# The PSUM tiles of a woven attention and Fourier stage in other banks

## The chip, the cores and the metric

The kernel runs on one core of a Trainium2 chip. The metric is the device time of one execution in microseconds (us); smaller is better. "Before" is the kernel as it stands, "after" the same kernel with the change described below.

## The reference, cut to what matters

Two results are put side by side in the output. Part A is a segmented attention with a memory (32 heads of width 18, four segments of 512 positions); part B takes the real part of a two-dimensional Fourier transform, written as products with cosine and sine matrices.

```
q, k, v = x @ wq, x @ wk, x @ wv           # [2048, 576], 32 heads x 18, 4 segments x 512
for each segment s:
    a_dot = softmax(causal(q_s k_s^T * 18**-0.5)) @ v_s
    a_mem = (phi(q_s) @ M) / (phi(q_s) @ z + 1e-6)
    out_s = sigmoid(beta) * a_mem + (1 - sigmoid(beta)) * a_dot
    M += phi(k_s)^T v_s ;  z += sum phi(k_s)
A = out @ wo
B = Cr @ (xB @ Hr^T) - Ci @ (xB @ Hi^T)    # [2048, 576]
result = concat(A, B)
```

## The kernel before, in words

The kernel has three stages, and the order of the instructions on each engine is the order in which the program records them (no scheduler moves them). Float32 operands are split into a high and a low half, so that a product takes three matmuls for each block of 128.

**Stage 1** (the loop over `s`, four segments) makes q, k and v of each segment, looks up the memory and adds to it. Its PSUM pool takes all eight banks. Banks 0 to 2 hold the sums of the memory (`m_ps`); they are read for the last time by `memory()` at the start of the last segment (L372, L374) and stand empty from there on. The five other banks, 3 to 7, are five buffers of one tag, `acc`, taken in turn by the products of q, k (L250, L84), v (L84) and by the lookups.

A lookup (`lookup(s, j)`, one for each of the four position tiles `j` of a segment) uses two of these banks. The first one, `o`, takes nine small matmuls (L396), goes to SBUF by ACT (L397) and is read a last time by DVE (L407). The second one, `u`, takes three matmuls (L402 to L404), is read by ACT (L405, L406) and by DVE (L408 to L410), and then serves as scratch for the denominators: DVE adds 1e-6 (L413), takes the reciprocal (L414) and multiplies by the gate (L415). Only when L415 has run is the bank free. GpSimd then forms the result (L417).

**Stage 2**, the woven stage, opens a second PSUM pool when the first one is closed. Its tiles wait for what used their bank before, tile by tile (`reuse_waits="tile"`), and not for the whole pool. It weaves two streams into one: `dense()`, the Fourier products, and `attention()`, which is cut into eight slots per pair of heads with a planned length each (`SLOTS`). After every slot of the attention the loop draws so many Fourier products that both streams get through at the same rate.

- Fourier: `hidden(ri, tt)` (L622 to L627) makes one product of 14 matmuls for each half of the columns, into a tile `d` of 128 x 288. Three banks take turns for `d`. ACT takes the high half out (L628), and one tick later DVE the low half (recorded at L94, since it is put off with `later`). `product()` and `sequence()` (matmuls at L577) come after the 16 tiles of `hidden`. The operands are cut from a loaded chunk: ACT makes `chi` (L451) and `xtail` (L453); one tick later `clo` (L456) and the low part of `xtail` (L458) are made, by GpSimd, except for the first two chunks, which DVE does.
- Attention: `scores` (L738) fills a tile `s` for a pair of rows of the score matrix, and `smallest` masks it and finds the largest score (L744: a custom DVE instruction, followed by a small one that reads its accumulator). `s` has two banks in turn (`s0`, `s1`), `t` two (`t0`, `t1`) and `pv` one.

The program thus takes its first steps in stage 2 in this order on PE: the first score of head 0 (512 columns), the first `d` product of 14 matmuls, six matmuls of the second `d` product, the second score of head 0 (two matmuls of 128 and 384 columns), the eight matmuls left of the second product, the third score (256 columns), the third and fourth `d` products (14 matmuls each, chunk 1), and then the fifth (chunk 2, whose `clo` is GpSimd's).

Which bank a tag gets is settled when a tile of it is first made: the pool gives the lowest free ones. Before the change the two lines ahead of `EDGE` make two `s` tiles that nobody uses, so that `s` comes first. The built program has them so; the right column tells the last user of the bank in stage 1 and its last reader:

| bank | before | last user in stage 1, last reader |
|---|---|---|
| 0, 1, 2 | `s`, `s`, `d` (1st product) | sums of the memory, read at the start of segment 3 |
| 3 | `d` (3rd product) | v of tile 3, second half; DVE L327 |
| 4 | `d` (2nd product) | `u` of the lookup of tile 3, the last of the stage; DVE L415 |
| 5 | `t`, also `trm` | v of tile 3, first half; DVE L327 |
| 6 | `t` | `u` of the lookup of tile 2; DVE L415 |
| 7 | `pv` | `o` of the lookup of tile 3; DVE L407 |

## Time and profile before

| what | value |
|---|---|
| median of 3 runs | 1001.27 us (1000.71 to 1001.88) |
| the profiled execution's own time | 1002.62 us |
| DMA | 209 GB/s on average, 208.92 MB |
| share of the chain that ended last, by engine | PE 85%, DVE 5%, ACT 4% |

The profile is of one execution. Its span runs from the first to the last instruction and is 1.7 us shorter than the execution's own time (1002.62 - 1000.9). PE is the matmul engine, PEld its weight loads, DVE VectorE, ACT ScalarE, POOL GpSimd, SP the queue that issues nearly all DMAs. A row of the timeline gives the start in us from the start of the span, the duration, the engine, the line of the code and the tiles (written <- read); in brackets stands how long the engine was idle before, and what the profile takes for the end of that idle time.

### The profile page before, as it was taken

The numbers are of one execution on the slowest core, as the hardware profiler recorded it, in microseconds if no ns is written. First come the engines' busy times: TensorE is split into PE (matmuls) and PEld (weight loads), VectorE is DVE, ScalarE is ACT, GpSimd is POOL, SyncE is SP. The second block draws the span as 40 slices with busy tenths as digits, with TensorE's granted clock in tenths as the row PEclk, the third lists the DMA queues.
The fourth block names the chain that finished last, engine by engine and source line by source line (L and its number), as shares of the span: only waits on it lengthen the run. The fifth ranks groups of instructions, "written<-read, shape, count | busy, mean of one in ns | idle before, by whom it ended". The sixth has DMA issues, their size and how long they took to land.

```text
span 1000.9 us, 25591 instructions
## 1 busy us (share of the span) xinstructions
PE 990.0 (99%) x9294; PEld 925.6 (92%) x9294; DVE 752.7 (75%) x2052; ACT 712.3 (71%) x1680; POOL 635.9 (64%) x700
## 2 busy tenths in 40 slices
PE   9999999989999999999999999999999999999998
PEld 8989989889999999999999999999999999999998
DVE  6557667594678777878898888898888899998321
ACT  7757575653887787878778788877767777777243
POOL 2657576675767667666766776776767767767000
PEclk9999999999999999999999999999999999999999
DMA  7537456767588999899999987889999999989455
GB/s 248 185 117 252 178 176 244 233 231 217 143 186 211 219 240 227 203 236 220 249 220 238 218 218 191 180 203 233 226 227 213 233 237 247 248 188 200 127 150 139
DMA packets 305614, 208.92 MB, mean 209 GB/s; under 512 B 206288, under 2 KB 260432, under 8 KB 305488
## 3 DMA queue, kind: packets, MB, share of 16 engines
q1 hardware_dynamic: 305248, 207.15, 81.0%
q8 instruction: 73, 1.20, 0.5%
q14 instruction: 53, 0.43, 0.2%
q10 hardware_dynamic: 240, 0.14, 0.0%
HBM read 121.32 MB, written 57.93 MB: 179 GB/s over the span
## 4 chain that ended last, share of the span: by engine, by line
PE 85%; DVE 5%; ACT 4%; issue 2%; POOL 1%; DMA 1%; SPq 0%; POOLq 0%; DVEq 0%; ACTq 0%
PE d L577 38%; PE s L738 7%; PE d L84 6%; PE v L84 4%; PE pv L856 4%; PE qk L250 4%; PE d L622 3%; PE d L623 3%; PE d L624 3%; PE pv L857 2%; PE m L363 1%; PE t L812 1%; PE qk L84 1%; DMA craw<-cT 1%; DVE r L276 1%
## 5 line engine op out<-in xcount | busy, mean ns | idle before, releaser
L744 DVE CUSTOM_DVE_ANT_0 s<-s,causal 128x128 f32<-128x128 f32 (+3 forms) x512 | 249.7, 498 | 103.2 <-PE s L738 94.1
L456 POOL TENSOR_TENSOR clo<-craw,chi 128x512 fp32r<-128x512 f32 x158 | 216.8, 1372 | 100.0 <-ACT chi L451 73.1
L577 PE MATMUL d<-wide,chi 128*128 128x288 f32 x1408 | 266.2, 306 | 0.4 <-DVE y L647 0.4
L577 PEld LDWEIGHTS d<-wide,chi 128*128 128x128 f32 x1408 | 211.8, 189 | 3.2 <-issue 0.9
L577 PE MATMUL d<-wide,clo 128*128 128x288 f32 x704 | 177.5, 319 | 0.0
L778 POOL TENSOR_TENSOR hl<-pf,hl 128x768 f16<-128x768 f32 x64 | 112.9, 1764 | 68.6 <-ACT hl L774 55.3
L824 ACT ACTIVATE phi<-t 128x384 f16<-128x384 f32 x128 | 61.7, 482 | 103.4 <-PE t L821 103.3
L738 PE MATMUL s<-ks,qs 108*128 108x128 bf16 (+3 forms) x512 | 133.9, 304 | 1.3 <-ACT pf L767 0.8
L767 ACT ACTIVATE pf<-s,nb 128x128 f32<-128x128 f32 (+3 forms) x256 | 128.3, 527 | 6.2
L839 DVE TENSOR_TENSOR plo<-pf,phi 128x384 f16<-128x384 f32 (+1 forms) x128 | 126.4, 987 | 0.0
L577 PE MATMUL d<-ab,chi 128*128 128x288 f32 x640 | 126.0, 306 | 0.0
L577 PEld LDWEIGHTS d<-wide,clo 128*128 128x128 f32 x704 | 118.6, 189 | 1.6
L825 ACT ACTIVATE pf<-t 128x384 f32<-128x384 f32 (+1 forms) x192 | 99.5, 518 | 6.1 <-PE t L812 5.9
L451 ACT ACTIVATE chi<-craw 128x512 fp32r<-128x512 f32 x160 | 100.1, 626 | 4.1 <-DMA craw<-cT 2.2
L577 PEld LDWEIGHTS d<-ab,chi 128*128 128x128 f32 x640 | 98.5, 189 | 0.6
L774 ACT ACTIVATE hl<-pf 128x768 f16<-128x768 f32 (+1 forms) x128 | 87.4, 729 | 2.0
L622 PE MATMUL d<-wide,chi 128*128 128x288 f32 x256 | 84.8, 331 | 2.8 <-ACT xtail L453 2.8
L577 PE MATMUL d<-ab,clo 128*128 128x288 f32 x320 | 84.8, 314 | 0.0
L623 PE MATMUL d<-wide,chi 128*128 128x288 f32 x256 | 76.1, 297 | 0.0
L624 PE MATMUL d<-wide,clo 128*128 128x288 f32 x256 | 76.0, 297 | 0.0
L778 DVE TENSOR_TENSOR hl<-pf,hl 128x512 f16<-128x512 f32 x64 | 67.7, 1058 | 0.1
L839 POOL TENSOR_TENSOR plo<-pf,phi 128x384 f16<-128x384 f32 x64 | 59.4, 928 | 12.9 <-ACT pf L825 10.3
(214 smaller groups left out, 2500.0 us busy)
## 6 DMA issues: line engine op xcount, KB each, us to landing
craw<-cT SPq DMA_DIRECT2D x128, 256.0 KB
ks<-kd SPq DMA_DIRECT2D x32, 432.0 KB
qs<-qd SPq DMA_DIRECT2D x32, 432.0 KB
craw<-xtT SPq DMA_DIRECT2D x32, 320.0 KB
vd<-vs SPq DMA_DIRECT2D x16, 440.0 KB
vst<-vd SPq DMA_DIRECT2D x32, 220.0 KB
qd<-p SPq DMA_DIRECT2D x16, 384.0 KB
kd<-p SPq DMA_DIRECT2D x16, 384.0 KB
```

The costliest lines, as they stand in the source:

```text
L84: pe.matmul(o, a, b, start=n == 0, stop=n == len(terms) - 1)
L451: act.activation(hi, raw[:, :4], AF.Copy)
L456: engine.tensor_tensor(lo, raw[:, :4], hi.bitcast(F32), OP.subtract)
L577: pe.matmul(o[h], a, b[:, h * 288:h * 288 + 288], start=start, stop=stop)
L622: pe.matmul(o, xh[:, k], wl[k][:, cs], start=k == 0, stop=False)
L623: pe.matmul(o, xh[:, k], wh[k][:, cs], start=False, stop=False)
L624: pe.matmul(o, xl[:, k], wh[k][:, cs], start=False, stop=False)
L738: pe.matmul(o[:, c:c + w], q[:, i * P:w], k[:, :w], start=True, stop=True)
L744: dve.tensor_tensor_reduce(o[:, c:c + w], o[:, c:c + w], CAUSAL[0][:, L - w:], scale=scale, scalar=-LOWEST, op0=OP.add, op1=OP.min, accum_ ...
L767: act.activation(f[:, FIRST_COL[i]:FIRST_COL[i] + w], o[:, c:c + w], AF.Exp, bias=nb[:, i:i + 1], scale=-1.0)
L778: engine.tensor_tensor(hl[:, 1, a:b], f[:, a:b], hl[:, 0, a:b], OP.subtract)
L839: (pool if kind == 2 else dve).tensor_tensor(lo[:, a:b], f[:, a:b], hi[:, a:b], OP.subtract)
```

## The change

Unused tiles of the other tags are made ahead of the two unused `s` tiles, so that the pool hands out its banks in another order. Nothing else changes: the built program has the same instructions in the same order on every engine and in every queue.

```
+    ps.tile([P, 288], F32, name="d", bufs=3)
+    for tag in "tt":
+        bank("t", [P, L], F32, tag)
+    ps.tile([P, 448], F32, name="pv", bufs=1)
     for _ in range(2):
         bank("s", [P, L], F32, "s")
```

`bank` gives the two buffers of a tag in turn; since it is called twice for each tag, the turn afterwards is as it was. In the built program the banks then stand so: `d` in 0 (first product), 2 (second) and 1 (third), `t` in 3 (also `trm`) and 4, `pv` in 5, `s` in 6 (first score) and 7 (second score). The waits of five PE instructions differ:

| PE instruction | waited before for | waits after for |
|---|---|---|
| first score, its weight load | its operands' loads | those, and the last readers of bank 6 (ACT L406, DVE L415 of the lookup of tile 2) |
| second `d` product, first matmul | the last readers of bank 4 (ACT L406, DVE L415 of the lookup of tile 3) | nothing |
| second score, first matmul | nothing | the last reader of bank 7 (DVE L407 of the lookup of tile 3) |
| `trm`, at 243.7 us of the span | its operands | those, and a product of stage 1 on PE itself |
| a score after `trm` | nothing | a lookup of stage 1 on PE itself |

## The prediction

> **What bounds the kernel now.** The page first: the busy shares, and the granted clock in 40 slices.

> ```profile
> span 1000.9 us, 25591 instructions
> PE 990.0 (99%) x9294; PEld 925.6 (92%) x9294; DVE 752.7 (75%) x2052; ACT 712.3 (71%) x1680; POOL 635.9 (64%) x700
> PEclk9999999999999999999999999999999999999999
> ```

> PE is busy all the time and the next engine at 75%. So a change that gives PE the same instructions in the same order can move the end in two ways alone: by PE's waits, and by the speed at which its matmuls run. The waits of PE are few; the second view lists all of them.

> ```profile
> engine line waited for: us in total, times, longest us
> PE d L622 <- ACT xtail L453: 2.8, 1, 2.8
> PE warm L239 <- DVE ones L68: 1.1, 1, 1.1
> PE s L738 <- ACT pf L767: 0.8, 1, 0.8
> PE d L577 <- DVE y L647: 0.4, 1, 0.4
> PE s L738 <- DVE negm L744: 0.4, 2, 0.2
> PE kt L305 <- ACT kf L271: 0.4, 2, 0.2
> ```

> Half of what PE waits for is one wait, 2.8 us, before a Fourier product, and none is for a DMA. The timeline shows it at the seam of the two stages:

> ```profile
> 219.00 0.28 PE L404 MATMUL look<-md,pq_hi 128*128 128x152 f32 x1
> 219.11 0.39 PE L738 MATMUL s<-ks,qs 108*128 108x512 bf16 x1
> ...
> 220.94 0.30 PE L626 MATMUL d<-wide,xtail 128*128 128x288 f32 x1
> ...
> 221.07 0.29 PE L627 MATMUL d<-wide,xtail 128*128 128x288 f32 x1
> ...
> 222.25 0.20 DVE L407 TENSOR_TENSOR nd<-nd,look 128x57 f32<-128x57 f32 x1
> ...
> 223.78 0.30 ACT L453 ACTIVATE xtail<-craw 128x128 fp32r<-128x128 f32 x1
> ```

> ```profile
> 223.84 0.19 DVE L415 TENSOR_TENSOR w<-look,g 128x32 f32<-128x32 f32 x1
> ...
> 224.18 0.37 PE L622 MATMUL d<-wide,chi 128*128 128x288 f32 x1 [2.81 <-ACT xtail L453]
> ...
> 224.58 0.14 DVE L744 DVE_READ_ACCUMULATOR2_ANT negm<- 128x1 f32 x1
> ...
> 225.05 0.49 PE L738 MATMUL s<-ks,qs 108*128 108x128 bf16 x2
> ```

> The first product ends at 221.36 (221.07 + 0.29), the second one starts at 224.18. The profile names ACT's `xtail`, because that instruction ends last (224.08). But it is of the next chunk, which this product does not read. What the product waits for by the program is bank 4, and that is free when DVE's L415 ends, at 224.03. From there to PE's start are 0.15 us; I use that as the handoff to PE throughout.

> The second cost is in the table by stretches (last columns: granted clock, DMA share, GB/s):

> ```profile
> 224.00:225.00 1.00, 0.82 (x6) 0.83 (x6) 0.72 (x3) 0.08 (x1) 0.83 (x1) 1.00 0.00 0
> 225.00:226.00 1.00, 1.00 (x7) 0.95 (x6) 0.39 (x3) 0.00 (x0) 1.00 (x2) 0.61 0.07 16
> 226.00:227.00 1.00, 1.00 (x6) 1.00 (x5) 0.91 (x3) 0.00 (x0) 0.94 (x2) 0.50 0.78 288
> 227.00:228.00 1.00, 1.00 (x6) 0.85 (x6) 0.26 (x1) 0.41 (x1) 0.92 (x2) 0.50 0.65 253
> 228.00:229.00 1.00, 1.00 (x7) 1.00 (x7) 0.54 (x3) 0.00 (x0) 0.92 (x1) 0.68 1.04 225
> 229.00:232.00 3.00, 3.00 (x25) 3.00 (x23) 0.46 (x1) 1.20 (x4) 1.34 (x2) 1.00 0.94 293
> ```

> A microsecond after the gap the clock is at half speed, for 0.39 + 0.50 + 0.50 + 0.32 = **1.71 us** of lost full-speed time (the shares missing to 1.00). So the gap costs 2.81 + 1.71, about 4.5 us, 0.45% of the span. That is all that is at stake.

> **The change part by part.** Nothing is added, removed or moved on any engine or queue. Only waits change.

> *Removed: the wait of the second product.* Its new bank, 2, has been empty for the whole segment. PE would go on at 221.20 (221.07 plus the spacing of 0.13 that the rows at 220.94 and 221.07 show). For more matmuls I take the spacing from these two starts, 14 products apart:

> ```profile
> 229.86 0.29 PE L622 MATMUL d<-wide,chi 128*128 128x288 f32 x1
> ...
> 231.73 0.29 PE L622 MATMUL d<-wide,chi 128*128 128x288 f32 x1
> ```

> (231.73 - 229.86) / 14 = 0.1336 us, or 0.46 ns a column. 231.73 is also the start of the fifth product, the mark at which I compare.

> *Added: the first score waits for bank 6.* All of PE is queued behind it.

> ```profile
> 215.40 0.25 ACT L406 ACTIVATE nd<-look 128x76 f32<-128x76 f32 x1
> ...
> 217.41 0.19 DVE L415 TENSOR_TENSOR w<-look,g 128x32 f32<-128x32 f32 x1
> ```

> The bank's last readers end at 215.65 and 217.60, and the score starts at 219.11: met 1.5 us earlier. Cost 0; it would take a DVE late by more than 1.5 us to cost anything.

> *Added: the second score waits for bank 7.* Six matmuls of the second product run from 221.20 to 222.00. Then the score needs DVE's L407, which ends at 222.45; with the handoff PE starts at 222.60. **A wait of 0.60.** Behind it stand eight Fourier matmuls and everything else on PE. It can't be longer by much, since DVE's row does not depend on anything that moves, nor much shorter: 0.50 with a handoff of 0.05.

> *What is late next: the third score.* It waited for the reading of the first score already, and never had to. Now: 222.60 + 0.24 (512 columns) + 8 x 0.1336 = 223.91. But the first score's maximum is read by DVE at 224.58 to 224.72, behind the whole of the last lookup; plus 0.15 is 224.87. **A wait of 0.96.** So the two new waits together bring PE back to what held it before, DVE's queue; but by then PE is through with 14 products and two scores, where before it had done six products.

> *Then.* 224.87 + 0.12 (256 columns) + 28 x 0.1336 = 228.73 for the start of the fifth product. Its third matmul, at 229.00, needs `clo` of chunk 2 from GpSimd:

> ```profile
> 227.64 1.28 POOL L456 TENSOR_TENSOR clo<-craw,chi 128x512 fp32r<-128x512 f32 x1
> ```

> That ends at 228.92, and GpSimd's chain up to there hangs on L415, not on PE, so that it does not move: 229.07, **a wait of 0.07**. The fifth product in effect starts at 228.80, where before it was 231.73: **2.93 us earlier**. In terms of its causes: 2.81 less 1.63 of new waits is 1.2, and 1.7 is the clock, if it stays whole.

> The GpSimd term can be worse, as DVE now runs its masks and the first low half about 0.8 us sooner beside it. The nearest rows for such a meeting:

> ```profile
> 217.52 0.68 DVE L456 TENSOR_TENSOR clo<-craw,chi 128x512 fp32r<-128x512 f32 x1
> ...
> 219.41 1.64 DVE L456 TENSOR_TENSOR clo<-craw,chi 128x512 fp32r<-128x512 f32 x1
> ```

> The same instruction took 0.96 more where GpSimd's L336 ran beside it. What DVE moves here reads PSUM and ran beside GpSimd before as well, so I take 0 and keep 0.96 for the range; below nothing there is no reason. With handoffs of 0.05 in place of 0.15 at the three waits the gain is 0.3 more.

> *`trm` and the score behind it* wait for PE's own count, for products 20 us old. A count that PE has to look at by itself took this:

> ```profile
> L622 PEldq EVENT_SEMAPHORE  x1: 51/51/51, 224.1 to 224.1; - x1
> ```

> Here it rides on the matmul; 0 to 0.05 us each, and I take 0. Two such separate counts stand at the seam before and after.

> **Does it stay to the end?** No later wait of PE in the list is for a DMA, and where ACT cuts the chunks that feed PE it waited for the load only twice:

> ```profile
> ACT chi L451 <- DMA craw<-cT: 2.2, 2, 1.8
> ```

> All engines get their work about 3 us sooner, in the same order, so the other waits move along. Sum for the profiled execution: 1002.62 - 2.93 = 999.69 (span 1000.9 to about 998.0). The runs shown have a median 1.35 below it, so **1001.27 - 2.93 = 998.3 us**.

> **The rivals.**

> *The clock is cut all the same (B).* After the change PE rests 0.60 and 0.96 us within 2.9 us. For: the 2.81 us in one piece did it, with products running for the last microsecond before the cut. Against: the next longest wait within the run, 0.8 us, did not, and the mean granted clock says that no other did:

> ```profile
> core 0: 1000.9 us, clock 0.998
> ```

> (1 - 0.998) x 1000.9 is 2.0 us lost, and 1.71 of it are accounted for. 1.56 in two pieces lies nearer to 0.8 than to 2.81. If it is cut, 1.71 is lost among the 28 matmuls and the wait of 0.07 goes: gain 2.93 + 0.07 - 1.71 = 1.29, **1000.0 us**.

> *The timed runs before had no cut (C).* The cut began at 225.2, where nothing in the kernel happens. If its place is fixed by something outside, the gap may fall elsewhere in other executions. Then before itself reaches the fifth product at 224.18 + 0.07 (the slower first matmul) + 42 x 0.1336 + 0.36 = 230.22, and the gain is 230.22 - 228.80 = 1.42: **999.9 us**. The three runs before are 1.2 us apart, which neither shows nor excludes it.

> [...]

> *The gain is handed back (E).* PE is ahead of its loads for a while; if the DMA queue, at shares of 0.94 to 1.04 at 228 to 232 us, can't bring later chunks sooner, PE waits for them instead. Then up to 2.93 goes: **about 1001 us**. Against it: no wait for a DMA in the list, two in ACT's.

> *The new banks make each product slower (D, the other side).* If writing `d` next to banks that DVE and ACT read costs PE time, it does so for 780 us:

> ```profile
> 232.00:1000.00 768.00, 495.43 (x3072) 433.38 (x3072) 1.00 0.88 209
> ```

> That is L577 alone, 3072 matmuls: 1 ns each is 3.07 us, and from 0.95 ns on the gain is gone. At 2 ns, 1% of a product: +6.1 - 2.9 = +3.2, **1004.5 us**. Against it: products of the same size took the same time in banks 3 to 7 (v) as in 2 to 4 (`d`):

> ```profile
> L624 PE MATMUL d<-wide,clo 128*128 128x288 f32 x256 | 76.0, 297 | 0.0
> ...
> L84 PE MATMUL v<-wide,xl 128*128 128x288 f32 x128 | 37.7, 295 | 0.0
> ```

> **How the numbers follow.** Chances: forecast 0.62, B 0.11, C 0.14, E 0.08, D 0.05. The predicted time is the forecast's, 998.3. Its own bounds are 998.0 (handoffs) and 999.3 (GpSimd). To take in B and C the range goes up to 1000.0, and at both ends I add 0.5, the distance of the lowest run before from the median: **997.5 to 1000.5**. It leaves out D, E and a rest of the forecast. 0.2% (2.0 us, up to 999.27) is about what a measurement of this kernel can tell from no change. Faster by more: the forecast, 0.62. Within: B, C and E, 0.33. Slower: D, 0.05.

> **What would show it.** In the profile after: no wait of PE before the second `d` product; a wait of about 0.6 before the second score, for L407, and of about 1.0 before the third, for L744; PE's fifth product at about 228.8 of the span in place of 231.7; granted clock 1.00 in every stretch from 224 to 232. A stretch at 0.50 means B. PE waits for DMA, or a later `d` product without the lead of 2.9, mean E. More than 495 us for the 3072 matmuls of L577 means D. The prediction is wrong if PE's lead at the fifth product is under 2 us with a whole clock.

## The result, and the profile after

The median of after is 998.98 us (10 runs, 997.85 to 1001.78) beside 1001.28 us for before (10 runs on the same chip): 2.30 us less, a ratio of 0.9981 with the interval [0.9973, 0.9989]. Two further comparisons of the same pair gave 998.50 beside 1001.48 (0.9975 [0.9966, 0.9983]) and 998.26 beside 1000.95 (0.9973 [0.9964, 0.9983]). The gain is thus 2.3 to 3.0 us; the forecast was 2.93.

The profiled execution of after has an own time of 998.12 us. The page shows the span and PE's share, the second view lists PE's waits (total, times, longest):

```profile
span 996.4 us, 25591 instructions
PE 988.1 (99%) x9294; PEld 923.0 (93%) x9294; DVE 753.6 (76%) x2052; ACT 712.3 (71%) x1680; POOL 634.8 (64%) x700
```

```profile
PE s L744 <- DVE negm L750: 1.2, 3, 0.8
PE warm L239 <- DVE ones L68: 1.1, 1, 1.1
PE d L583 <- DVE y L653: 0.4, 1, 0.4
PE kt L305 <- ACT kf L271: 0.3, 2, 0.2
PE s L744 <- DVE nd L407: 0.3, 1, 0.3
```

The diff adds six lines, so that L744 is before's L738, L750 its L744, L628 its L622, L583 its L577. The wait of 2.8 us before the second product is gone. In its place stand the two waits that the prediction announced: one of 0.3 for L407, and one of 0.8 for the first score's maximum (among the three of the first row). The timeline at the seam has them in brackets:

```profile
218.65 0.39 PE L744 MATMUL s<-ks,qs 108*128 108x512 bf16 x1
...
220.61 0.30 PE L633 MATMUL d<-wide,xtail 128*128 128x288 f32 x1
...
220.74 0.30 PE L628 MATMUL d<-wide,chi 128*128 128x288 f32 x1
...
221.78 0.20 DVE L407 TENSOR_TENSOR nd<-nd,look 128x57 f32<-128x57 f32 x1
...
222.03 0.38 PE L744 MATMUL s<-ks,qs 108*128 108x128 bf16 x2 [0.33 <-DVE nd L407]
...
224.10 0.14 DVE L750 DVE_READ_ACCUMULATOR2_ANT negm<- 128x1 f32 x1
...
224.29 0.27 PE L744 MATMUL s<-ks,qs 108*128 108x256 bf16 x1 [0.82 <-DVE negm L750]
...
227.17 1.29 POOL L456 TENSOR_TENSOR clo<-craw,chi 128x512 fp32r<-128x512 f32 x1
...
228.14 0.30 PE L628 MATMUL d<-wide,chi 128*128 128x288 f32 x1
```

The second product starts 0.13 behind the last matmul of the first one (220.61, 220.74): it waits for nothing. The last row is the fifth product. From the first score to it after takes 228.14 - 218.65 = 9.49 us, before 231.73 - 219.11 = 12.62, so **3.13 less**. One product further on, at 230.26 beside 233.64, it is 2.92, since after loses 0.21 to `clo`; there it stays, to within 0.02, until 480 us.

The stretches of the same place show the clock (the column behind the five engines):

```profile
223.00:224.00 1.00, 0.47 (x4) 0.34 (x3) 0.97 (x3) 0.92 (x3) 0.31 (x1) 1.00 0.00 0
224.00:225.00 1.00, 0.70 (x6) 0.70 (x6) 0.97 (x5) 0.00 (x0) 1.00 (x2) 1.00 0.00 0
225.00:226.00 1.00, 1.00 (x9) 1.00 (x8) 1.00 (x6) 0.00 (x0) 1.00 (x1) 1.00 0.30 118
226.00:227.00 1.00, 1.00 (x10) 1.00 (x9) 0.26 (x2) 0.53 (x2) 0.94 (x2) 1.00 0.55 213
```

It is whole throughout, where before it stood at 0.61 and 0.50.

**The two profiled executions are 4.5 us apart (1002.62 and 998.12), and only 2.92 of it belong to the change.** The rest: 0.47 before the first score (the clock became whole at 3.98 us of the span in after and at 6.77 in before, by the trace's clock record, so that the first product of real data started 0.46 sooner); 0.82 at 525 us, where a score of before waited 0.84 for ACT's `pf` and in after did not; 0.27 at the end. In the twelve profiles of the experiments the wait at 525 us was there once (1.06, with the filler of 48). A difference of two profiles has to be read from mark to mark; the difference of their ends mixes the change with such chances.

### The profile page after: what moved, and what is told of

It reads as the page before. It is cut to its first block, busy times and chain, and to the rows that moved or that the text cites. A ratio compares the mean times of both kernels' runs of the same rounds, so it can differ in the third digit from the quotient of the medians.

```text
span 996.4 us, 25591 instructions
## 1 busy us (share of the span) xinstructions
PE 988.1 (99%) x9294; PEld 923.0 (93%) x9294; DVE 753.6 (76%) x2052; ACT 712.3 (71%) x1680; POOL 634.8 (64%) x700
## 4 chain that ended last, share of the span: by engine, by line
PE 86%; DVE 5%; ACT 4%; issue 2%; DMA 1%; POOL 1%; SPq 0%; POOLq 0%; DVEq 0%; ACTq 0%
PE d L583 39%; PE s L744 7%; PE d L84 6%; PE pv L862 4%; PE v L84 4%; PE qk L250 4%; PE d L628 3%; PE d L630 3%; PE d L629 3%; PE pv L863 2%; PE m L363 1%; PE t L818 1%; PE qk L84 1%; PE t L821 1%; DVE r L276 1%
## 5 line engine op out<-in xcount | busy, mean ns | idle before, releaser
L750 DVE CUSTOM_DVE_ANT_0 s<-s,causal 128x128 f32<-128x128 f32 (+3 forms) x512 | 249.8, 498 | 100.9 <-PE s L744 91.8
L456 POOL TENSOR_TENSOR clo<-craw,chi 128x512 fp32r<-128x512 f32 x158 | 216.3, 1369 | 95.4 <-ACT chi L451 69.4
L583 PE MATMUL d<-wide,chi 128*128 128x288 f32 x1408 | 266.3, 306 | 0.4 <-DVE y L653 0.4
L583 PEld LDWEIGHTS d<-wide,chi 128*128 128x128 f32 x1408 | 211.8, 189 | 2.4 <-DVE y L653 0.6
L583 PE MATMUL d<-wide,clo 128*128 128x288 f32 x704 | 177.6, 319 | 0.0
L744 PE MATMUL s<-ks,qs 108*128 108x128 bf16 (+3 forms) x512 | 133.7, 304 | 1.7 <-DVE negm L750 1.2
L583 PE MATMUL d<-ab,chi 128*128 128x288 f32 x640 | 125.9, 306 | 0.0
L583 PEld LDWEIGHTS d<-wide,clo 128*128 128x128 f32 x704 | 118.6, 189 | 1.6
L451 ACT ACTIVATE chi<-craw 128x512 fp32r<-128x512 f32 x160 | 100.1, 626 | 3.7 <-PE d L583 1.4
L583 PEld LDWEIGHTS d<-ab,chi 128*128 128x128 f32 x640 | 98.5, 189 | 0.6
L583 PE MATMUL d<-ab,clo 128*128 128x288 f32 x320 | 84.8, 314 | 0.0
L628 PE MATMUL d<-wide,chi 128*128 128x288 f32 x256 | 84.0, 328 | 0.0
```

The source lines that it names most:

```text
L451: act.activation(hi, raw[:, :4], AF.Copy)
L456: engine.tensor_tensor(lo, raw[:, :4], hi.bitcast(F32), OP.subtract)
L583: pe.matmul(o[h], a, b[:, h * 288:h * 288 + 288], start=start, stop=stop)
L628: pe.matmul(o, xh[:, k], wl[k][:, cs], start=k == 0, stop=False)
L744: pe.matmul(o[:, c:c + w], q[:, i * P:w], k[:, :w], start=True, stop=True)
L750: dve.tensor_tensor_reduce(o[:, c:c + w], o[:, c:c + w], CAUSAL[0][:, L - w:], scale=scale, scalar=-LOWEST, op0=OP.add, op1=OP.min, accum_ ...
```

## The experiments

The lead below is the time from the first score to the sixth product, compared with the 14.53 us of before (233.64 - 219.11). It leaves out what an execution gained or lost ahead of the seam, and in the three profiles of after it was 2.91 or 2.92. "Cut" counts timed runs whose mean granted clock was 0.998 or less: 3.41 us at half clock, as in before, take 0.0017 off the mean. Where in a run the cut lay only its profile tells.

| kernel | median us | before beside it | ratio and interval | lead in the profile | cut |
|---|---|---|---|---|---|
| after, again | 998.50 | 1001.48 | 0.9975 [0.9966, 0.9983] | 2.91 | 0 of 11 |
| `d` first, scores where DVE is late | 1001.46 | 1001.48 | 1.0006 [0.9996, 1.0017] | 1.85, but first score 3.27 late | 8 of 11 |
| filler in the gap (48) | 1000.29 | 1001.48 | 0.9994 [0.9986, 1.0003] | 1.53 | 0 of 11 |
| three products first | 998.54 | 1001.48 | 0.9973 [0.9964, 0.9982] | 2.91, later 1.14 | 0 of 11 |
| denominators in SBUF | 998.78 | 1001.03 | 0.9980 [0.9971, 0.9988] | 2.62 | 1 of 11 |
| after, chunk load early | 998.10 | 1001.03 | 0.9970 [0.9959, 0.9982] | 2.90 | 0 of 6 |
| three products first, relieved | 998.02 | 1001.03 | 0.9968 [0.9959, 0.9978] | 4.02, later 2.62 | 0 of 9 |
| filler, 6 matmuls | 1001.15 | 1001.02 | 1.0000 [0.9991, 1.0009] | 1.54 | 10 of 11 |
| filler, 12 matmuls | 1000.67 | 1001.02 | 0.9993 [0.9984, 1.0001] | 0.00 | 7 of 11 |
| after, second product whole | 998.40 | 1001.02 | 0.9971 [0.9960, 0.9981] | 2.92 | 0 of 7 |
| after, beside the next | 998.26 | 1000.95 | 0.9973 [0.9964, 0.9983] | 2.91 | 0 of 9 |
| chunk load early, beside after | 998.07 | 1000.95 | 0.9971 [0.9960, 0.9983] | 2.90 | 0 of 6 |

Of the 90 timed runs of before in these comparisons 83 were cut. Their median is 1001.12, that of the seven others 999.67.

### After, again

No edit.

> The changed kernel once more, beside the others on the same chip. Its ten runs so far are spread over 3.9 us (997.85 to 1001.78), those of before over 1.3. Theory (the seam decides, and in some executions the clock is cut once more): the profile has waits of PE of 0.3 before the second score and 0.8 before the third, the runs with a clock of 1.00 or 0.999 lie near 998, those with 0.998 or 0.997 about 1.7 us higher. Rival (PE's lead of 3 us is lost to something later in some executions): runs near 1000.5 with a whole clock.

The second profile has the same two new waits, and the lead is the same to 0.01. None of the eleven runs is cut, so that the theory's figure for cut runs is not tested here. The rival's sign is there, though: two of the eleven lie at 1000.29 and 1000.83 with a clock of 1.00 and 0.999, and one of the first ten lies at 1000.55 with 1.00. None of these three was profiled, so what they lost, and where, is open. In the three profiles of after the lead is not lost.

### `d` first: one part of the change alone

The Fourier products get the empty banks, as in after; but the scores then get banks 3 and 4, which DVE reads late, and not 6 and 7.

```
+    ps.tile([P, 288], F32, name="d", bufs=3)
     for _ in range(2):
         bank("s", [P, L], F32, "s")
```

> One part of the change alone: only the tiles of d are made ahead of those of s, so that d has banks 0 to 2, the first score bank 3 and the second score bank 4 (last read by L415). Rival (any layout with d in the empty banks brings the gain): as after, 2.3 us under before. Theory (every bank that is taken early must be free early): the first score waits for DVE's L327 on bank 3, about 3.2 us, with all of PE behind it; the fifth product starts at 230.5 of before's time base with a whole clock (1.2 us under before) and at 232.2 with the cut that a gap of this size has brought (0.5 us over before). Theory's forecast: 0 to 0.8 us over before.

PE's longest wait from the list, and then two rows of the timeline:

```profile
PE s L739 <- POOL mb L483: 3.2, 1, 3.2
```

```profile
221.46 0.82 DVE L327 TENSOR_TENSOR vr<-v,vs 128x288 f32<-128x288 f32 x2
...
222.38 0.59 PE L739 MATMUL s<-ks,qs 108*128 108x512 bf16 x1 [3.15 <-POOL mb L483]
```

The wait has moved from the second product to the first score, and all of the gain is gone. The profile names GpSimd's `mb`, which the score has nothing to do with; bank 3 comes free with L327, which ends at 222.28, 0.10 ahead of the score. So it is not the empty banks as such that gain: the tile that comes next on PE has to be given the bank whose reader is done. The clock was cut for longer here, for 6.83 us (221.63 to 228.46).

### Filler in the gap: the clock by itself

Before, with 48 matmuls ones x ones of 128 columns after the first product, into the bank of the second score. The wait's end is not touched.

```
+    def filler(n):
+        o = ps.tile([P, L], F32, name="fill", tag=f"s{turns['s'] ^ 1}", bufs=1)
+        for _ in range(n):
+            pe.matmul(o[:, :P], ones, ones, start=True, stop=True)
...
+                if ri == tt == 0:
+                    filler(48)
```

> Before, with 48 small matmuls (ones times ones, 128 columns, into the bank of the second score, which is empty until then) put between the first and the second Fourier product: PE is kept busy in the gap, the wait for L415 stays. They add work, and leave the result as it is. Theory (the stretch at half clock comes from the gap): clock whole at 225 to 229, fifth product at about 230.2 in place of 231.7, time 1.5 us under before. Rival (the stretch has another cause): clock 0.50 in that stretch as before, time as before or up to 0.2 over.

```profile
223.00:224.00 1.00, 0.89 (x10) 0.74 (x7) 0.88 (x3) 0.24 (x2) 0.66 (x1) 1.00 0.00 0
224.00:225.00 1.00, 1.00 (x10) 0.93 (x10) 0.35 (x2) 0.00 (x0) 1.00 (x2) 1.00 0.00 0
225.00:226.00 1.00, 1.00 (x10) 0.93 (x9) 0.97 (x5) 0.29 (x1) 0.94 (x2) 1.00 0.64 247
```

With PE kept busy the clock stays whole in this execution (1.00 in every stretch from 223 to 226, where before had 0.61 and 0.50 from 225 on), and the sixth product comes 1.53 us sooner though the second one starts as far behind the first score as before. That is the clock's share. In the timed runs the median is 1.2 below before, with an interval that reaches just over 1; the profile carries the verdict here.

The same profile shows that an execution can lose such a lead later. It is 2.36 ahead of before's place in the span behind the seam, 1.57 at 526 us and 0.58 at PE's last matmul (it ends at 995.54, before's at 996.12); part of that are its wait of 1.06 at 525 us and two of 0.2 in the last products. Its own time was 1001.91, the longest of its eleven runs.

### Filler of 6 and of 12: when the clock is cut

The same edit with `filler(6)` and `filler(12)`, so that the wait is 2.45 and 2.11 us long and ends where it did.

> Before with 6 matmuls ones x ones of 128 columns after the first product, into the bank of the second score, so that the wait before the second product shrinks by about 0.4 us to some 2.4 us; the end of the wait stays where it was. Theory (the clock is set in windows of 3.41 us that run freely from before the kernel; a window in which PE rests for more than a share between 1.52 and 2.37 us is followed by one at half speed): whether the clock is cut differs from execution to execution with the place of the windows, fewer runs are cut than of before, and a cut costs 1.7 to 1.9 us of that run: median 999.5 to 1001.3. Rival (the length of the gap in one piece decides, with a bound between 1.71 and 2.81 us): all runs are cut (time as before) or none is (about 1.5 us less).

> The same with 12 matmuls: a wait of some 2.1 us. Theory (windows): few or no runs are cut, since at most 2.1 us of rest can fall into one window; median 999.3 to 1000.3. Rival (length in one piece): all or none, as with 6.

The two waits from the timeline, each followed by the stretches around it, first of the kernel with 6 matmuls:

```profile
223.48 0.37 PE L627 MATMUL d<-wide,chi 128*128 128x288 f32 x1 [2.45 <-ACT xtail L453]
```

```profile
223.00:224.00 1.00, 0.52 (x4) 0.55 (x5) 0.97 (x4) 0.38 (x2) 0.53 (x1) 1.00 0.00 0
224.00:225.00 1.00, 1.00 (x10) 0.93 (x10) 0.24 (x2) 0.00 (x0) 1.00 (x2) 1.00 0.09 16
```

and the one with 12:

```profile
223.51 0.38 PE L627 MATMUL d<-wide,chi 128*128 128x288 f32 x1 [2.11 <-ACT xtail L453]
```

```profile
223.00:224.00 1.00, 0.49 (x3) 0.52 (x4) 0.97 (x4) 0.41 (x2) 0.49 (x1) 0.87 0.00 0
224.00:225.00 1.00, 1.00 (x6) 0.85 (x6) 0.06 (x1) 0.00 (x0) 1.00 (x2) 0.50 0.06 16
...
227.00:228.00 1.00, 1.00 (x8) 0.89 (x8) 0.45 (x3) 0.41 (x1) 1.00 (x1) 0.92 1.12 324
```

The clock's fall at the very end, first of before and then of the kernel with 12:

```profile
1000.00:1001.00 1.00, 0.00 (x0) 0.00 (x0) 0.00 (x0) 0.00 (x0) 0.00 (x0) 0.52 0.00 0
```

```profile
998.00:999.00 1.00, 0.00 (x0) 0.00 (x0) 0.00 (x0) 0.00 (x0) 0.00 (x0) 0.78 0.00 0
```

In these two executions the longer wait left the clock whole, and the shorter one cut it: a bound on the length of one gap can't give that, and the rival falls. Windows of a fixed length can. That length is in the clock record of before's trace: whole from 6.77 us of the span, half from 225.22, whole again from 228.63, half from 1000.04, for the rest after the last instruction on PE. The slow stretch lasted 3.413 us. From 6.77 to 225.22 it is 218.45 us, which is 64 times 3.4133, and from one fall to the other 774.82 us, which is 227 times 3.4133. After has two changes, at 3.98 and 993.84: 989.86 us, 290 times 3.4133. In the kernel with 12 the clock falls at 223.74 (0.87 = 0.74 + 0.26 / 2) and is whole again at 227.16, 3.42 us later; to the fall at the end it is 998.57 - 223.74 = 774.83, as in before; with `d` first it is 999.87 - 221.63 = 778.24, 228 times 3.4133. So the changes of each of these four executions lie on a grid of its own of 3.413 us. Counting it back from the fall at the end gives each execution's windows, and PE's rest in them; that the rest in the window ahead of a grid point decides is the theory, and the last two columns fit it:

| execution | window ahead of the grid point | the wait | its part in the window | clock |
|---|---|---|---|---|
| before | 221.81 to 225.22 | 221.36 to 224.18 | 2.37 | cut |
| `d` first | 218.22 to 221.63 | 219.23 to 222.38 | 2.40 | cut |
| filler of 12 | 220.33 to 223.74 | 221.40 to 223.51 | 2.11 | cut |
| denominators in SBUF | 221.19 to 224.61 | 221.00 to 222.70 | 1.51 | whole |
| filler of 6 | 218.95 to 222.36 to 225.78 | 221.03 to 223.48 | 1.33 and 1.12 | whole |
| after | 222.43 to 225.84 | 223.47 to 224.29 | 0.82 | whole |

Read so, the bound lies between 1.51 and 2.11 us of rest in one window of 3.41 in these six executions. The end of after narrows it: PE's last matmul ends at 991.88 and the clock falls at 993.84, with 1.96 us of rest in the window. So it lies between 1.51 and 1.96 here. A wait of 2.81 nearly always brought a cut (83 of 90 runs), one of 2.45 mostly (10 of 11), one of 2.11 often (7 of 11), one of 1.71 hardly ever (1 of 11). The one of 3.15, with `d` first, brought it in 8 of 11, so at these counts the order is not strict.

Of my numbers for the two medians one held, 999.5 to 1001.3 for 6 (1001.15); 999.3 to 1000.3 did not for 12 (1000.67), since I had expected few runs to be cut there. With 6 I had expected fewer cut runs than of before, and 10 of 11 beside 21 of 23 is no fewer.

The cost of a cut at this place is the difference of the two: with 6 the lead is 1.54, with 12 it is 0.00, the second product starting at the same place after the first score in both. In the timed runs of before it is 1001.12 - 999.67 = 1.45, in those of the kernel with 12 (seven cut, four not) 1001.00 - 999.20 = 1.80. I had expected 1.7 to 1.9; the profiles say 1.54.

### Denominators in SBUF: who releases the bank

Before, with the same banks; only the scratch of the lookup leaves PSUM.

```
-        den = u[:, 456:456 + H, None]
+        den = sb.tile([P, H, 1], F32, name="den", bufs=2)
```

> Before, with one edit: the lookup's denominators stand in a tile of SBUF and not in the PSUM tile u. Bank 4 is then free when DVE's L410 ends (223.15 in the trace of before) and not when L415 does (224.03). Theory (the second product waits for the bank's last DVE reader, whatever the profile names; the clock is cut by the length of the gap): the second product starts at about 223.2 after a wait of about 1.85 us, so 1.0 us sooner. If a gap of 1.85 us leaves the clock whole, the fifth product starts 2.5 to 2.7 us sooner and the time falls like that of the change, to within 0.5 us of it; if the clock is cut all the same, the gain is 1.0 or less. Rival (the releaser is ACT's xtail, as the profile says): the product starts at 224.18 as before and the time stays.

The first fence is of the timeline, the second one of the stretches:

```profile
222.25 0.31 DVE L410 TENSOR_TENSOR nd<-nd,look 128x152 f32<-128x152 f32 x1
...
222.66 0.62 ACT L451 ACTIVATE chi<-craw 128x512 fp32r<-128x512 f32 x1
...
222.70 0.37 PE L622 MATMUL d<-wide,chi 128*128 128x288 f32 x1 [1.71 <-DVE nd L410]
```

```profile
224.00:225.00 1.00, 1.00 (x10) 0.93 (x9) 0.97 (x7) 0.00 (x0) 1.00 (x2) 1.00 0.00 0
225.00:226.00 1.00, 1.00 (x10) 1.00 (x9) 1.00 (x5) 0.41 (x1) 0.94 (x2) 1.00 0.44 170
```

The product starts when L410 has read the bank, long before ACT has made the `xtail` that the profile of before had named; 1.10 us sooner than before by the first score. The wait of 1.71 leaves the clock whole, 1.10 and the 1.53 of the clock give the lead of 2.62 to within 0.01, and one line of code gains about what the change gains (0.9980 [0.9971, 0.9988]). That settles both open points of its expectation: the releaser is L410, and the time falls like that of the change. That the length of the gap by itself cuts the clock, as its theory has it, no run shows: 2.45 us left it whole and 2.11 cut it, with 6 and with 12 matmuls.

### Three products first

After, with three Fourier products drawn ahead of the second score.

```
-        while td / total_d < ta / total_a:
+        while td / total_d < ta / total_a or td < 3 * 14 * HM:
```

> After, with three Fourier products drawn ahead of the second score, so that neither the second nor the third score has to wait for DVE. Rival (DVE's queue is the only thing that is late at the seam now): the two waits of 0.3 and 0.8 go and the time falls by another 1.1 us. Theory (GpSimd is next: its clo of chunk 2 ends at 228.9 of before's time base and hangs on L415): the waits before the scores go, but a wait of about 1.5 us for GpSimd's L456 appears before the third matmul of the fifth product, which then starts in effect no sooner than in after; time as after within 0.3 us.

PE's two new waits, and a row of ACT's timeline:

```profile
PE trm L801 <- POOL mb L797: 1.6, 1, 1.6
PE d L630 <- POOL clo L456: 1.4, 1, 1.4
```

```profile
237.98 0.63 ACT L451 ACTIVATE chi<-craw 128x512 fp32r<-128x512 f32 x1 [3.39 <-DMA craw<-xtT]
```

The two new waits of after are gone, and the fifth product has a lead of 4.59. But `clo` is not ready sooner, and at the sixth the lead is 2.91 again; then ACT waits 3.39 us for the load of chunk 5, GpSimd gets `mb` done late behind that chunk, and PE waits 1.6 more before `trm` (the lead is 1.14 behind it). This is rival E of the prediction: it is real, and in the profiles it begins only when PE runs further ahead than the change brings it.

### Chunk load early, alone and with three products first

After, with two lines more where a chunk is taken:

```
     def chunk(n):
         c_load(n + 4)
+        if n == 0:
+            c_load(5)
```

> After, with chunk 5's load issued on SP ahead of the loads of vst, ks and qs that follow chunk 0. Theory (PE is bound by its own work from the seam on, and ACT's wait of 1.07 us for this load at 236 us is hidden): ACT's wait goes, PE's starts up to 500 us stay as in after within 0.1 us of the seam's mark, the time is that of after within 0.5 us. Rival E (part of the gain is handed back to the loads in many executions): the time falls by 0.7 us or more under that of after, and its scatter shrinks.

> After with the early load of chunk 5 once more. Theory (that load is hidden behind PE's work): within 0.3 us of after in this comparison. Rival E (part of the gain is handed back to the load in many executions): 0.4 us or more under after, as the two medians of different comparisons have it (998.10 beside 998.50 and 998.98).

> After itself once more, to stand beside the early load of chunk 5 on the same chip: 998.0 to 999.0 by the runs so far.

The edit did less than its text says. SP's rows show chunk 5's load, first in after and then with the edit:

```profile
228.38 0.44 SPq L94 DMA_DIRECT2D qs<-qd  x1
228.92 2.33 SPq L441 DMA_DIRECT2D craw<-xtT  x3
```

```profile
228.43 0.38 SPq L441 DMA_DIRECT2D craw<-xtT  x1
228.86 0.39 SPq L94 DMA_DIRECT2D qs<-qd  x1
```

It passed `qs` alone and was issued 0.49 us sooner. ACT's cut of this chunk, in the same order:

```profile
236.09 0.63 ACT L451 ACTIVATE chi<-craw 128x512 fp32r<-128x512 f32 x1 [1.07 <-DMA craw<-xtT]
```

```profile
234.92 0.62 ACT L451 ACTIVATE chi<-craw 128x512 fp32r<-128x512 f32 x1
```

ACT's wait is gone there (in the second profile with the edit it was still 0.83), and PE's lead is 2.90 either way; side by side the medians are 998.07 and 998.26, 0.19 apart. The load is hidden behind PE's work, as the theory has it; the 0.4 to 0.9 between medians of different comparisons is thus not shown to be an effect of it.

With three products first, the early load, and GpSimd's memset of the `ks` stacks put off by six ticks:

```
-    def stacks(p_, i):
+    def stacks(p_, i, wait=0):
...
-        pool.memset(ks_bufs[i].bitcast(F32)[96:], BF16_ONES)
+        later(wait, pool.memset, ks_bufs[i].bitcast(F32)[96:], BF16_ONES) if wait else pool.memset(ks_bufs[i].bitcast(F32)[96:], BF16_ONES)
...
-                stacks(sa, p + 2)
+                stacks(sa, p + 2, 6)
```

> After, with three of Fourier products drawn ahead of the second score (as in the run with three products first), chunk 5's load issued early, and GpSimd's memset of the ks stacks put off by six ticks. Theory (in the run with three products first, GpSimd's clo cost 1.4 us and the load of chunk 5 cost 1.6 us of wait before trm; both are met here): the wait for clo falls to about 0.5 us, the one before trm goes, and the time is 1 to 2.5 us under that of after. Rival (the lead at this place is given back to whatever comes next, DVE's scores or a later load): as after within 0.5 us.

```profile
PE trm L803 <- POOL mb L799: 1.2, 1, 1.2
...
PE d L632 <- POOL clo L456: 0.3, 1, 0.3
```

The wait for `clo` fell to 0.3 (I had expected 0.5), the one before `trm` only to 1.2: ACT still waited 3.02 us for the same load. Counted from the first score, the load was issued at 9.82 us beside 10.32 without the edit, and ACT's cut of the chunk started at 18.28 beside 19.76. So the edit brought it sooner, but not soon enough for a PE that is 4.02 ahead. The time of 1 to 2.5 us under after did not come: 998.02 us is the lowest median of all, but 0.08 from the early load alone beside it and near those of after (998.26 to 998.98), and the lead after `trm`, 2.62, is below after's. The rival (the lead goes to whatever comes next) held, and I do not call it faster than after.

### Second product whole ahead of the second score

```
-        while td / total_d < ta / total_a:
+        while td / total_d < ta / total_a or td < 2 * 14 * HM:
```

(with the early load of chunk 5)

> After, with chunk 5's load issued early, and the second Fourier product drawn whole ahead of the second score (14 products instead of 6 there). Theory (the new waits are DVE's queue, so work put ahead of the scores covers them): the wait for L407 (0.33) goes, the one for the first score's maximum (0.82) shrinks to under 0.6, the wait for clo before the fifth product takes back what is gained up to about 0.5, and the time is that of the run with the early load alone, 0 to 0.6 us less. Rival (chunk 5's load comes later again and is waited for, as with three products first): a wait before trm, and a time above that of the early load alone.

```profile
224.41 0.27 PE L746 MATMUL s<-ks,qs 108*128 108x256 bf16 x1 [1.30 <-DVE negm L752]
```

I had this half wrong. The wait for L407 went, but the one for the maximum did not shrink; it grew from 0.82 to 1.30, and the lead is 2.92. The third score starts when DVE has read the first one, at the same place in both (5.64 and 5.66 us after the first score); work that is only shifted in front of it shifts the rest, and does not take it away.

## Why the prediction was right, step by step

- **The wait of the second product goes.** Right, and so was the reading against the profile's releaser: the run with the denominators in SBUF puts PE's start at the bank's last reader on DVE.
- **First score no wait.** Right.
- **Second score 0.60, third 0.96.** The releasers were right, the sizes in the profile 0.33 and 0.82. Some 0.16 of each is only where one counts from: the profile counts from the end of the last matmul (a row of 0.29), and I from where the next could start (0.13 behind its start). Counted my way they are 0.49 and 0.98. The term that was mis-sized is the handoff: L407 ends at 221.98 and PE starts at 222.03, `negm` ends at 224.24 and PE starts at 224.29. It is 0.05, the lower value that the prediction named, and not the 0.15 that I took from 224.03 to 224.18. The third wait keeps its size, since both its ends come 0.1 sooner; at the fifth product the lead is 3.13 where I had 3.00. The 0.15 fits the wait that it was read from: with the denominators in SBUF it is 0.14 there (222.56 to 222.70). In before PE has a row for a count that it looks at by itself ahead of that product (0.05 long, at 224.1), and in after it has none ahead of the two new waits.
- **`clo` 0.07.** Mis-sized. GpSimd's row ends where it should (228.46, as far behind the first score as before), and PE goes on 0.05 later, at 228.51; but the next matmul follows 0.24 behind this one (228.75) and not 0.13: 0.21 in all.
- **The clock 1.71.** Right in kind: its cut comes from the gap (filler), and it is whole in after. The size was a little too big: a cut costs 1.54 of PE's time and not 1.71. The step that was off is to take the clock's missing share for lost time, as if matmuls started twice as far apart at half clock. Before's rows there are 0.24 apart, 1.80 times the 0.1336 at full clock:

```profile
225.58 0.44 PE L623 MATMUL d<-wide,chi 128*128 128x288 f32 x1
225.82 0.44 PE L624 MATMUL d<-wide,clo 128*128 128x288 f32 x1
226.06 0.44 PE L622 MATMUL d<-wide,chi 128*128 128x288 f32 x1
```

  By them 3.41 us at half clock cost 3.41 x (1 - 0.1336 / 0.24) = 1.51.
- **The sum.** Forecast 2.93 at the seam, measured 2.92: 1.54 by the clock and 1.38 by the waits, where I had 1.71 and 1.22. By steps, the handoffs brought 0.13 more than forecast and `clo` took 0.14 more. These errors cancel by luck; the sum is closer than its parts deserve.
- **It stays to the end.** Right: 2.91 at 240 us (so `trm` took nothing) and at 480 us. PE's last matmul ends 4.24 sooner (991.88 beside 996.12), which is the 0.46 before the first score, the 2.92 and the 0.84 at 525 us to within 0.02.
- **The transfer to the median.** The timed gains are 2.30, 2.98 and 2.69. Since 83 of 90 runs of before are cut and 28 of 30 of after are not, the change is worth in nearly all runs what it was worth in the profile. Runs without a cut have medians of 999.67 (seven runs only) and 998.41, 1.26 apart; the waits' 1.38 agrees.
- **Rival B (cut all the same)** came in 2 of 30 runs of after, at 1000.99 and 1001.78. What made PE rest long enough in those I can't see, as neither was profiled.
- **Rival C (no cut in the runs before)** had the right condition, in that the grid of the clock's changes stands at another place in each execution's span (its first change at 6.77 in before, 3.98 in after), and too high a chance: 7 of 90 runs. The price that I gave it, a gain of 1.42, fits the 1.26.
- **Rival E** takes nothing in the three profiles of after, and begins with three products first. Whether it took something in the three runs of after near 1000.5 with a whole clock is open.
- **Rival D (the other side)** is out by one row, the same group as in before, of after:

```profile
232.00:1000.00 768.00, 495.43 (x3072) 433.38 (x3072) 1.00 0.87 209
```

3072 products in other banks take 495.43 us, to the hundredth what they took.

## What to carry to other kernels

When a pool of PSUM tiles follows another one without a break, list for each bank when its last reader ends, and give the banks that are free first to the tiles that come first on the engine that sets the end; a scratch tile that stays in PSUM counts as a reader, and moving it out can be worth as much as a new layout (here 2.25 us, 1001.03 to 998.78, beside 2.3 to 3.0). Take the releaser of a wait from the program, not from the profile, when several instructions end close together. Price a gap on PE with the clock as well as by its own length: here a cut cost 1.5 us more, and in the six executions of the table above it came where more than some 1.5 to 2.0 us of rest fell into one window of 3.41.
